# Retention, soft mixture of experts and a gated MLP in one kernel: the weights' place among the loads, and the keys' transposes

## The chip, the cores and the metric

The kernel runs on one core of a Trainium2 chip. The metric is the time of one execution on the device in microseconds (us), the median of three runs. The engines are called PE (TensorE, matrix products and transposes), DVE (VectorE), ACT (ScalarE), POOL (GpSimd) and SP (SyncE, which here issues most DMA loads).

## The reference

Three stages, one feeding the next. A linear attention with decay (4 batches, 8 heads, 768 tokens, 64 columns a head) gives 3072 tokens of 512 columns. A soft mixture of 8 experts with 4 slots each mixes all tokens into 32 slots, runs the experts and mixes back. An MLP of width 2048 follows.

```python
for t in range(S):
    state = gamma * state + einsum('bhd,bhe->bhde', k[:, :, t], v[:, :, t])
    y[:, :, t] = scale * einsum('bhd,bhde->bhe', q[:, :, t], state)
logits = x @ phi
d = softmax(logits, axis=0); slot_input = d.T @ x
slot_out[e] = maximum(slot_input[e] @ w1[e], 0) @ w2[e]
x = softmax(logits, axis=1) @ slot_out
h = x @ w_in
out = (h * sigmoid(1.702 * h)) @ w_out
```

## The kernel before

The order of all work is written out by hand: each engine runs its instructions in the order of the program, and waits only for what it reads or overwrites. Memory comes from pools of tiles; an instruction that takes a tile over waits until its last users are done.

**Chunks.** The tokens are worked in 24 chunks of 128 (6 to a batch). Chunk i has a load of 768 KB (`load_a`: keys, queries and values, tensor kqv) that SP issues in `loads(i - 4)`, four chunks ahead, into one of five rotating buffers; so it also waits until chunk i - 5 has released its buffer (its last product with the queries, L266). The steps of a chunk are `stage_a` (scores, L206), `stage_p` (mask, on DVE), `stage_v` (two products on POOL, vt and tb), and `stage_b`: the output y on PE (L266 and L270), the state (L278, copied by ACT to s_sb), and the product of y and tb on DVE, xT (L282). All chunks share one y tile of two PSUM banks; `stage_b` uses the first 256 columns of each bank. Chunks come in pairs; after `stage_b(i - 1)` of an odd i comes `group(i)`, which holds transposes of earlier chunks (`stage_c`, L291), and in turn logits, softmax statistics and slot sums of four chunks at a time.

**Keys.** For the state the keys are needed the other way round. For most chunks ACT's queue loads them a second time (tensor kt, 256 KB each, `load_b`); for chunks 4, 9, 14 and 19 (`KTP`) PE transposes them in `keys` (called in the groups of i = 3, 9, 13 and 19), into columns 256 to 511 of the y tile's two banks (`keys_tok`, L227), and ACT copies them out (L232). The next `stage_b` writes y anew and so waits for that copy.

**Weights.** The experts' weights are 32 pieces of 1 MB, loaded in the order of their use, some in halves. Among the chunks `loads(i)` asks for as many halves as a quota says, `(i - 1) * 2 * (NW + NQ) // (NI - 1)` with NW = 14, NQ = 3, NI = 24, ahead of the chunk load of the same call; what is left of the 17 pieces is asked for after the last chunk. Six more pieces follow into memory that the chunks release, and nine into buffers that the first expert products release. All are issued by SP in the order of the program. Two loads of the last stage are put among the last pieces (`early_loads`, keyed by the number of pieces left, `WL`): half of the first w_in tile when three are left, and half of the first w_out pair when two are left. Behind the last piece come the second w_in half, the second w_out half, and the next w_in tile.

**Experts and the start of the last stage.** `exp_w1`, `exp_t1`, `exp_w2`, `exp_t2`, `exp_sum` work one pair of experts: two products on PE (L512, L543) with a transpose between, ACT's copy of the result (os, L546), its transposes (tq, L552), ACT's th (L558) and two sums on DVE (A, L561). A feeds `make_gd` (L569), the first product with w_in, and by it all of the last stage. The last stage wants weights in another form: `narrow` makes three DVE operations (L157, L159, L161) of each part that lands, and for w_out `wout_ops` adds a rounding on ACT (L614) and a difference on POOL (L617). `f0_ops` and `f1_ops` are these five for the first two blocks of w_out, `w1_ops` the three for the second half of the first w_in tile; they stand between the expert steps at the places seen in the code.

**phi** (64 KB, for the logits) is loaded from POOL's queue at the start.

Of the kernel before, what the change touches and what calls it, by code (L numbers as in the profile page):

```python
# [24 lines left out]
NI = B * NC  # L25
# [6 lines left out]
CB = {"end": 160}  # L32
NB = NT // 512
NW = 14
NQ = 3
# [11 lines left out]
PAD = 128  # L47
BUD = 2.0
E0 = (1.2, 1.7, 1.7, 1.7, 2.2)
WL = (3, 2)  # L50


@with_exitstack
def retention_soft_moe_mlp(
# [12 lines left out]
    nc = tc.nc  # L67
# [42 lines left out]
    phi = at.tile([P, KDM, NS], F32, name="phi")  # L110
# [12 lines left out]
    def load_half(pool):  # L123
        if half:
            t, src = half.pop()
            nc.sync.dma_start(out=t[:, 2:4], in_=src[:, 2:4])
            return
        kind, e, k = pieces.pop()
        t = pool.tile([P, 4, 512], F32, tag="w", name=f"{kind}_{e}_{k}")
        src = (w1 if kind == "w1" else w2)[e, k, :, 0:2048].rearrange("p (j f) -> p j f", j=4)  # L130
        nc.sync.dma_start(out=t[:, 0:2], in_=src[:, 0:2])
        W[kind, e, k] = t
        half.append((t, src))

    def load_piece(pool, tag="w"):
        kind, e, k = pieces.pop()
        t = pool.tile([P, 4, 512], F32, tag=tag, name=f"{kind}_{e}_{k}")
        src = (w1 if kind == "w1" else w2)[e, k, :, 0:2048].rearrange("p (j f) -> p j f", j=4)
        nc.sync.dma_start(out=t, in_=src)
        W[kind, e, k] = t  # L140

    def load_wout(r, a0=0, a1=2):
        if a0 == 0:
            wo_t[r] = wq.tile([P, 2, DM], U64, tag="w", name=f"wo{r}")
        src = w_out[r].rearrange("p (a d) -> p a d", a=2)
        nc.sync.dma_start(out=wo_t[r][:, a0:a1], in_=src[:, a0:a1])

    def load_win2(j, z, f0=0, f1=256):
        if f0 == 0:
            raw_t[j, z] = wq.tile([P, KDM, 256], U64, tag="w", name=f"wi{j}_{z}")  # L150
        src = w_in[j, :, 1024 * z:1024 * z + 1024].rearrange("p (k f) -> p k f", k=KDM)
        nc.sync.dma_start(out=raw_t[j, z][:, :, f0:f1], in_=src[:, :, f0:f1])
# [135 lines left out]
    def stage_c(i):  # L288
        xp = mt([P, DM], f"xp{i}")
        for a in range(NP):  # L290
            nc.tensor.transpose(xp[:, a * P:(a + 1) * P], xT_t[i][:, a, :], ident)  # L291
        x_t[i] = xp
        if i < NI - 2:
            stage_c2(i)
# [15 lines left out]
    def logits(g):  # L310
        lp = mt([P, P], f"lp{g}")
        js = [range(4)] if g < NG - 1 else [range(3), range(3, 4)]
        for k, j in [(k, j) for js_ in js for k in range(KDM) for j in js_]:
            mm(lp[32 * j:32 * j + 32, :], lhsT=phi[:, k, :], rhs=xT_t[4 * g + j][:, k, :],  # L314
               start=(k == 0), stop=(k == KDM - 1))
        return lp
# [17 lines left out]
    def softmax_stats(g, lp):  # L334
        m, nm = softmax_max(g, lp)
        eT, es = softmax_exp(lp, nm, g)
        al = softmax_scale(g, nm)
        if g < NG - 1:
            keep_logits(g, lp)
        run["m"] = m  # L340
        g_t[g] = (eT, es, al)
# [22 lines left out]
    def stage_g2(g):  # L364
        eT, es, al = g_t[g]
        er = mt([P, 2, P], f"er{g}")
        if g < NG - 2:
            nc.tensor.transpose(er[:, 1], lT_t.pop(g), ident)
        e = exp_tr(g, eT, er[:, 0])
        run_z(es, al, g)  # L370
        g_t[g] = (e, al)
        return er[:, 1]
# [7 lines left out]
    def stage_g3(g):  # L380
        add_op(g, *slot_product(g))
# [28 lines left out]
    def row_softmax(g, rl):  # L410
        lp = rl.rearrange("p (j s) -> p j s", j=4)
        rx = sm.tile([P, 4], F32, tag="rx", name=f"rx{g}")
        nc.vector.reduce_max(out=rx, in_=lp, axis=AX.X)
        ce = sm.tile([P, 4, NS], F32, tag="eT", name=f"ce{g}")
        nc.vector.tensor_tensor(out=ce, in0=lp, in1=rx[:, :, None].to_broadcast([P, 4, NS]), op=ALU.subtract)
        ex = sm.tile([P, 4, NS], F32, tag="ex", name=f"ex{g}", bufs=1)
        nc.scalar.activation(out=ex, in_=ce, func=AF.Exp)
        return ex
# [434 lines left out]
    with tc.manual_schedule():  # L853
# [5 lines left out]
        nc.scalar.dma_start(out=ca_t[:, 0:CA["tab"]], in_=ca[:, 0:CA["tab"]])  # L859
        nc.scalar.dma_start(out=cb_t, in_=cb[:, 0:CB["end"]])  # L860
        nc.scalar.dma_start(out=ca_t[:, CA["tab"]:CA["end"]], in_=ca[:, CA["tab"]:CA["end"]])
        nc.gpsimd.dma_start(out=phi.rearrange("p k s -> p (k s)"), in_=cb[:, CB["end"]:CB["end"] + 128])
        wz = xx.tile([P, NP * P], F32, tag="xT", name="wz", bufs=5)
        nc.vector.memset(wz, 0.0)
        wu = ps.tile([P, NP * P], F32, tag="m", name="wu")
# [6 lines left out]
        ex_t, count = {}, [0]  # L872

        def group(i):
            spare["n"] = 0
            g = (i - 5) // 4
            if i % 4 == 1:
                if g > 0:
                    stage_g3(g - 1)
                lp = logits(g)  # L880
                keys(i)
                softmax_stats(g, lp)
                stage_c(i - 3)
            else:
                if i > 3:
                    spare["n"] = 1
                    rl = stage_g2(g)
                stage_c(i - 3)
                keys(i)
                if 3 < i < NI - 1:  # L890
                    ex_t[g] = row_softmax(g, rl)
            stage_c(i - 2)

        def keys(i):
            for x in (i, i + 1):
                if x in KTP:
                    keys_tok(x, y_p[0])

        def loads(i):
            if i >= NI:  # L900
                return
            while count[0] < (i - 1) * 2 * (NW + NQ) // (NI - 1):
                if i < 6 or half:
                    load_half(wp if count[0] < 2 * NW else wq)
                    count[0] += 1
                else:
                    load_piece(wp if count[0] < 2 * NW else wq)
                    count[0] += 2
            load_b(i + 1)
            for x in range(2 if i == 0 else i + 4, i + 5):  # L910
                load_a(x)

        for i in range(3):
            stage_a(i)
            stage_p(i)
            stage_v(i)
            loads(i)
            if i != 1:
                stage_b(max(i - 1, 0))
        for i in range(3, NI, 2):  # L920
            stage_a(i)
# [52 lines left out]
        xk, xk_e = pool(right, "xk", 2)  # L974
        slotT = xk.tile([P, KDM, NS], F32, name="slotT", bufs=1)
        slot_inputs(sb)
        early_loads = {WL[0]: lambda: load_win2(0, 0, 0, 128), WL[1]: lambda: load_wout(0, 0, 1)}
        while len(pieces) > 1:
            early_loads.get(len(pieces), lambda: None)()
            load_piece(wp)  # L980
        early_loads.get(1, lambda: None)()
        load_half(wp)
        load_half(wp)
        load_win2(0, 0, 128, 256)
        load_wout(0, 1, 2)
        load_win2(0, 1)
# [50 lines left out]
                )  # L1037
        exp_w2(2)
        f0_ops, f1_ops = wout_ops(0), wout_ops(1)
        for fn in f0_ops[0:3]:  # L1040
            fn()
        exp_w2(3, 0, 1)
        exp_sum(2, exp_t2(2))
        for fn in f0_ops[3:5]:
            fn()
        exp_w2(3, 1, 3)
        exp_w2(3, 3, 4)
# [304 lines left out]
```

## Time and profile before

| | us |
|---|---|
| median of three runs | 442.68 |
| the three runs | 442.94, 442.44, 442.68 |
| the profiled execution | 443.33 |
| its span, first to last instruction | 441.6 |
| PE busy | 429.5 |
| DVE busy | 329.5 |
| ACT busy | 213.8 |
| POOL busy | 72.4 |

The profile is of one execution. Busy times are sums over the span; they say how full an engine is, not what ends last at a given point. The chunks take the first 106 us, the experts run to 149 us, and the rest is the last stage. The granted clock of TensorE is full throughout.

### The profile page before, as it was taken

The numbers are of one execution on the slowest core, as the hardware profiler recorded it, in microseconds if no ns is written. First come the engines' busy times: TensorE is split into PE (matmuls) and PEld (weight loads), VectorE is DVE, ScalarE is ACT, GpSimd is POOL, SyncE is SP. The second block draws the span as 40 slices with busy tenths as digits, with TensorE's granted clock in tenths as the row PEclk, the third lists the DMA queues.
The fourth block names the chain that finished last, engine by engine and source line by source line (L and its number), as shares of the span: only waits on it lengthen the run. The fifth ranks groups of instructions, "written<-read, shape, count | busy, mean of one in ns | idle before, by whom it ended". The sixth has DMA issues, their size and how long they took to land.

```text
span 441.6 us, 10084 instructions
## 1 busy us (share of the span) xinstructions
PE 429.5 (97%) x4145; PEld 363.2 (82%) x4145; DVE 329.5 (75%) x627; ACT 213.8 (48%) x392; POOL 72.4 (16%) x83
## 2 busy tenths in 40 slices
PE   7999999989999999999999999999999999999995
PEld 5888888867433687888788879999999999999994
DVE  2547578564476689878968768698889999898835
ACT  2322332313121566566556556665666666665630
POOL 3453434432000123120131120000000000000000
PEclk9999999999999999999999999999999999999999
DMA  8999999999999767845683262402333333312102
GB/s 316 414 394 415 410 411 413 409 414 413 401 412 404 280 208 271 282 177 191 200 182 108 84 96 102 138 31 66 96 97 96 95 96 97 96 39 61 49 0 95
DMA packets 26109, 94.48 MB, mean 214 GB/s; under 512 B 2496, under 2 KB 9920, under 8 KB 20816
## 3 DMA queue, kind: packets, MB, share of 16 engines
q1 hardware_dynamic: 20704, 82.45, 50.0%
q0 software_dynamic: 2784, 7.41, 6.6%
q10 hardware_dynamic: 2576, 3.99, 2.5%
q8 instruction: 32, 0.52, 0.5%
q14 instruction: 13, 0.11, 0.1%
HBM read 79.16 MB, written 14.68 MB: 213 GB/s over the span
## 4 chain that ended last, share of the span: by engine, by line
PE 89%; DMA 8%; DVE 1%; issue 0%; ACT 0%; POOL 0%; SPq 0%; DVEq 0%; POOLq 0%
PE pb L814 32%; PE pb L746 25%; DMA kqv<-kqv_dram 7%; PE y L270 4%; PE sc L206 3%; PE hp L512 3%; PE eo L543 3%; PE pb L788 3%; PE pb L697 2%; PE y L266 2%; PE xp L291 2%; PE lp L314 1%; PE st L278 1%; PE op L393 1%; DMA kqv_first<-kqv_dram 1%; PE pb L579 1%
## 5 line engine op out<-in xcount | busy, mean ns | idle before, releaser
L814 PE MATMUL pb<-wb,ghl 128*128 128x256 f32 x672 | 100.9, 283 | 0.0
L814 PEld LDWEIGHTS pb<-wb,ghl 128*128 128x128 f32 x672 | 89.5, 192 | 0.1
L746 PE MATMUL pb<-wo_hl,gh 128*128 128x512 f32 x288 | 89.5, 395 | 0.0
L814 PE MATMUL pb<-wa,ghl 128*128 128x256 f32 x504 | 78.9, 283 | 0.0
L814 PEld LDWEIGHTS pb<-wa,ghl 128*128 128x128 f32 x504 | 68.7, 192 | 0.0
L746 PEld LDWEIGHTS pb<-wo_hl,gh 128*128 128x128 f32 x288 | 53.8, 188 | 11.8 <-ACT gh L706 0.2
L803 DVE TENSOR_TENSOR ghl<-F,ghl 128x896 fp32r<-128x896 f32 x56 | 60.7, 1084 | 0.0
L791 ACT ACTIVATE F<-pb 128x512 f32<-128x512 f32 x56 | 33.5, 599 | 52.3 <-PE pb L788 52.3
L746 PE MATMUL pb<-wo_hl,gl 128*128 128x512 f32 x144 | 55.9, 395 | 0.3 <-DVE gl L712 0.3
L799 ACT CAST ghl<-F 128x896 fp32r<-128x896 f32 x56 | 52.3, 934 | 0.9 <-DVE F L795 0.8
L712 DVE TENSOR_TENSOR gl<-gg,gh 128x512 fp32r<-128x512 f32 x36 | 24.7, 687 | 14.3 <-ACT gg L707 14.2
L706 ACT ACTIVATE gh<-pb 128x512 fp32r<-128x512 f32 x36 | 21.7, 604 | 26.9 <-PE pb L697 26.4
L793 DVE TENSOR_TENSOR F<-F 128x256 f32<-128x256 f32 x56 | 23.5, 420 | 14.0 <-ACT F L791 13.8
L282 DVE TENSOR_TENSOR xT<-y,tb 128x512 f32<-128x512 f32 x19 | 13.1, 691 | 27.0 <-PE y L270 27.0
L746 PEld LDWEIGHTS pb<-wo_hl,gl 128*128 128x128 f32 x144 | 27.0, 188 | 6.9 <-DVE gl L712 0.7
L280 ACT COPY s_sb<-st 128x256 f32<-128x256 f32 x20 | 7.5, 373 | 50.6 <-PE st L278 46.8
L219 DVE TENSOR_TENSOR pt<-sc,ca_t 128x512 f32<-128x512 f32 x44 | 28.2, 681 | 4.9 <-PE sc L206 4.9
L246 POOL TENSOR_TENSOR tb<-ca_t 128x512 f32<-128x512 f32 x19 | 19.9, 1048 | 42.7 <-DVE xT L282 42.7
L270 PE MATMUL y<-pt,vt 128*64 128x128 f32 x352 | 24.1, 279 | 0.0
L788 PE MATMUL pb<-cT,gst 128*128 128x256 f32 x112 | 22.8, 285 | 0.4 <-ACT gst L594 0.4
L206 PE MATMUL sc<-kqv 64*128 64x128 f32 x288 | 19.6, 281 | 3.0 <-DMA kqv<-kqv_dram 2.7
L270 PEld LDWEIGHTS y<-pt,vt 128*64 128x64 f32 x352 | 18.8, 136 | 3.6 <-issue 2.2
(197 smaller groups left out, 657.6 us busy)
## 6 DMA issues: line engine op xcount, KB each, us to landing
w<-w_dram SPq DMA_DIRECT2D x27, 1024.0 KB, 11.9
kqv<-kqv_dram SPq DMA_DIRECT2D x18, 768.0 KB, 9.9
wi<-w_in_dram SPq DMA_DIRECT2D x7, 1024.0 KB, 5.1
wo<-w_out_dram SPq DMA_DIRECT2D x7, 1024.0 KB, 5.0
scr<-sg POOLq DMA_DIRECT2D x28, 256.0 KB, 4.6
pr<-scr SPq DMA_DIRECT2D x12, 512.0 KB, 4.9
w<-w_dram SPq DMA_DIRECT2D x10, 512.0 KB, 12.5
out_dram<-X SPq DMA_DIRECT2D x10, 512.0 KB, 3.9
```

The lines of the kernel that those rows point to most:

```text
L206: mm(sc[hh][:, a, :], lhsT=kT[hh * D:(hh + 1) * D, a, :], rhs=q_[hh * D:(hh + 1) * D, a, :], start=True, stop=True)
L219: nc.vector.tensor_tensor(out=pt[hh], in0=sc[hh], in1=mask[:, None, :].to_broadcast([P, NP, P]), op=ALU.mult)
L270: mm(out_(a, hh ^ (a & 1)), lhsT=vt[:, 2 * a + (hh ^ (a & 1)), :], rhs=pt[hh ^ (a & 1)][:, a, :], start=(c == 0 and a < 2), stop=True, ski ...
L706: nc.scalar.activation(out=gh, in_=hp, func=AF.Gelu_apprx_sigmoid)
L712: nc.vector.tensor_tensor(out=gl, in0=gg, in1=gh.bitcast(F32), op=ALU.subtract)
L746: mm(acc[t], lhsT=g[:, t * P:(t + 1) * P], rhs=w, start=first and n == 0, stop=n == 2 and (last or final or (u == NSEQ - 2 and t == 3)))
L788: mm(hp[:, 256 * z:256 * z + 256], lhsT=gst[:, (f + z) * P:(f + z + 1) * P], rhs=cT[:, 256 * blocks[e]:256 * blocks[e] + 256], start=z == ...
L791: nc.scalar.activation(out=F[:, 0:4].rearrange("p q t -> p (q t)"), in_=hp, func=AF.Gelu_apprx_sigmoid)
L793: tt(out=F[:, 4:6], in0=F[:, 0, None].to_broadcast([P, 2, P]), in1=F[:, 1:3], op=ALU.subtract)
L799: nc.scalar.copy(out=GHL[k][:, 0], in_=F_[k][:, 1:8])
L803: nc.vector.tensor_tensor(out=GHL[k][:, 1], in0=F_[k][:, 1:8], in1=GHL[k][:, 0].bitcast(F32), op=ALU.subtract)
L814: mm(pv[:, p], lhsT=ghl[:, n // 2, g], rhs=wf[:, n % 2], start=j == j0[e] and n == 0 and i in (4, 0), stop=j == NSP - 1 and n == 2, skip_g ...
```

## The change

Five edits. The quota for weights among the chunks is taken from 15 pieces in place of 17; the pieces left over are asked for after the last chunk, so that their order is the same. phi's load moves from the start to behind the POOL work of chunk 1. In `group`, `keys` is the first step in place of standing after the logits, or after `stage_g2` and the first `stage_c`. The load of the first half of the first w_out pair moves from ahead of the last two expert pieces to behind them. The three DVE operations on it move from ahead of the first part of the last expert product to behind the sum of expert pair 2, where the rounding on ACT and the difference on POOL already stood.

```diff
-WL = (3, 2)
+WL = 3
...
-        nc.gpsimd.dma_start(out=phi.rearrange("p k s -> p (k s)"), in_=cb[:, CB["end"]:CB["end"] + 128])
...
             g = (i - 5) // 4
+            keys(i)
             if i % 4 == 1:
                 if g > 0:
                     stage_g3(g - 1)
                 lp = logits(g)
-                keys(i)
                 softmax_stats(g, lp)
                 stage_c(i - 3)
             else:
...
                 stage_c(i - 3)
-                keys(i)
                 if 3 < i < NI - 1:
...
-            while count[0] < (i - 1) * 2 * (NW + NQ) // (NI - 1):
+            while count[0] < (i - 1) * 2 * (NW + NQ - 2) // (NI - 1):
...
             loads(i)
-            if i != 1:
+            if i == 1:
+                nc.gpsimd.dma_start(out=phi.rearrange("p k s -> p (k s)"), in_=cb[:, CB["end"]:CB["end"] + 128])
+            else:
                 stage_b(max(i - 1, 0))
...
-        early_loads = {WL[0]: lambda: load_win2(0, 0, 0, 128), WL[1]: lambda: load_wout(0, 0, 1)}
+        early_loads = {WL: lambda: load_win2(0, 0, 0, 128)}
         while len(pieces) > 1:
             early_loads.get(len(pieces), lambda: None)()
             load_piece(wp)
-        early_loads.get(1, lambda: None)()
         load_half(wp)
         load_half(wp)
+        load_wout(0, 0, 1)
         load_win2(0, 0, 128, 256)
...
         f0_ops, f1_ops = wout_ops(0), wout_ops(1)
-        for fn in f0_ops[0:3]:
-            fn()
         exp_w2(3, 0, 1)
         exp_sum(2, exp_t2(2))
-        for fn in f0_ops[3:5]:
+        for fn in f0_ops[0:5]:
             fn()
         exp_w2(3, 1, 3)
```

## Rows read from the trace of the kernel before

**Rows 1.** The page, part 1: busy us (share of the span) x instructions.
```profile
PE 429.5 (97%) x4145; PEld 363.2 (82%) x4145; DVE 329.5 (75%) x627; ACT 213.8 (48%) x392; POOL 72.4 (16%) x83
```

**Rows 2.** The waits of PE: who waited for whom, us, times, longest.
```profile
PE sc L206 <- DMA kqv<-kqv_dram: 2.7, 3, 2.2
...
PE y L266 <- ACT kt L232: 0.6, 2, 0.3
```

**Rows 3.** Timeline of PE: start us, us, instruction, idle before and its releaser.
```profile
86.49 0.67 PE L266 MATMUL y<-kqv,s_sb 64*64 64x128 f32 x16 [0.32 <-ACT kt L232]
...
91.90 1.16 PE L206 MATMUL sc<-kqv 64*128 64x128 f32 x16 [2.16 <-DMA kqv<-kqv_dram]
```

**Rows 4.** Windows: busy us by engine; then granted clock, DMA share, GB/s.
```profile
56.00:106.00 50.00, 47.33 (x868) 39.95 (x864) 32.50 (x65) 14.46 (x42) 21.04 (x21) 1.00 1.02 412
104.00:148.00 44.00, 43.61 (x447) 19.19 (x445) 23.92 (x78) 9.86 (x24) 3.31 (x4) 1.00 1.00 403
```

**Rows 5.** Timeline of PE, the instructions at the head of the groups.
```profile
20.20 0.63 PE L227 MATMUL y<-cb_t,kqv_first 128*128 128x128 f32 x4
...
42.90 1.06 PE L393 MATMUL op<-x,e 128*32 128x512 f32 x8
...
59.08 1.06 PE L393 MATMUL op<-x,e 128*32 128x512 f32 x8
...
84.43 0.33 PE L368 MATMUL er<-cb_t,lT 128*128 128x128 f32 x1
```

**Rows 6.** Timeline of DVE, its reads of y before those groups.
```profile
19.43 0.69 DVE L282 TENSOR_TENSOR xT<-y,tb 128x512 f32<-128x512 f32 x1 [2.10 <-PE y L270]
...
42.62 0.69 DVE L282 TENSOR_TENSOR xT<-y,tb 128x512 f32<-128x512 f32 x1 [0.52 <-PE y L270]
...
58.78 0.67 DVE L282 TENSOR_TENSOR xT<-y,ca_t 128x512 f32<-128x512 f32 x1
...
84.08 0.69 DVE L282 TENSOR_TENSOR xT<-y,ca_t 128x512 f32<-128x512 f32 x1 [0.65 <-PE y L270]
```

**Rows 7.** Line 232, 42.9 to 44 us: ACT's wait, ns min/median/max, first and last start.
```profile
L232 ACTq EVENT_SEMAPHORE  x1: 256/256/256, 43.1 to 43.1; - x1
```

**Rows 8.** DMA issues at 63.2, 131.4, 131.9 and 150.1: KB each, us to landing.
```profile
kqv<-kqv_dram SPq DMA_DIRECT2D x1, 768.0 KB, 10.0
...
w<-w_dram SPq DMA_DIRECT2D x1, 512.0 KB, 13.6
...
wi<-w_in_dram SPq DMA_DIRECT2D x1, 512.0 KB, 14.3
...
wo<-w_out_dram SPq DMA_DIRECT2D x1, 1024.0 KB, 4.8
```

**Rows 9.** Timeline of SP, the issues of the first three.
```profile
63.17 0.33 SPq L178 DMA_DIRECT2D kqv<-kqv_dram  x1
...
131.12 0.43 SPq L126 DMA_DIRECT2D w<-w_dram  x1
131.92 0.38 SPq L152 DMA_DIRECT2D wi<-w_in_dram  x1
```

**Rows 10.** Timeline of DVE at the end of the experts.
```profile
142.27 0.42 DVE L157 TENSOR_SCALAR fr<-wo 128x512 uint32<-128x512 uint32 x1
...
143.45 0.69 DVE L161 SCALAR_TENSOR_TENSOR fr<-wo,fr 128x512 uint32<-128x512 uint32 x1
...
146.25 0.55 DVE L157 TENSOR_SCALAR win<-wi 128x512 uint32<-128x512 uint32 x1 [1.23 <-DMA wi<-w_in_dram]
148.43 0.36 DVE L561 TENSOR_TENSOR A<-tq,th 128x64 f32<-128x64 f32 x2 [1.63 <-ACT th L558]
```

**Rows 11.** Timeline of ACT in the same stretch.
```profile
144.54 0.62 ACT L614 CAST wo_hl<-fr 128x512 fp32r<-128x512 f32 x1
146.81 0.85 ACT L546 ACTIVATE os<-eo,zr 128x256 f32<-128x256 f32 x2 [1.66 <-PE eo L543]
```

**Rows 12.** Timeline of PE in the same stretch: the last expert product.
```profile
144.32 2.80 PE L543 MATMUL eo<-w,hT 128*32 128x256 f32 x48
```

## The prediction

> **What bounds the kernel now.** I read the page's first part, then the waits of TensorE (PE), then the windows, then the DMA loads one by one. The page gives PE 429.5 us of a 441.6 us span [rows 1], so a gain has to come out of the 12.1 us in which PE is idle, or out of PE work removed. The change removes none: it reorders. Of the idle time the waits name two kinds that the change touches: 2.7 us in three waits for the chunks' input (kqv), and 0.6 us in two waits for ScalarE's copy of transposed keys [rows 2]. The longest of the first, 2.16 us, stands at 91.9 us, and one of the second, 0.32 us, at 86.5 [rows 3].
>
> The windows show the second limit: the DMA engines are full (share 1.00 to 1.02, 403 to 412 GB/s) from the chunks to 148 us, when the experts end [rows 4]. So up to there bytes land on a timetable that no reordering of the asking speeds up; a transfer can only change places with another. At 412 GB/s a 1 MB piece takes 2.5 us, a half 1.27, a chunk's 768 KB 1.9.
>
> **1. Fewer weights among the chunks' loads.** The quota falls from 34 halves spread over the chunks to 30; by the two formulas chunk 18 is asked for behind 16 halves, not 20, and chunk 22 behind 22, not 26: 2 MB, 5.0 us earlier each. Before, chunk 18 was asked for at 63.17 and landed 10.0 us later [rows 8, 9]. All three kqv waits are shorter than one piece (2.5 us), which is the least that the chunks waited for move up, so all go: **-2.7 us** at PE. Bounds: 0 to -2.7.
>
> What is late next is the queue itself: it may run dry. Chunk 18 is asked for when a buffer comes free, paced by PE. Alone in the queue a 1 MB load took 4.8 us [rows 8], that is 2.3 us of head and 2.5 of transfer; so before, chunk 18 stood behind 10.0 - 2.3 - 1.9 = 5.8 us of transfers once its head was over. With 5.0 us of weights gone and PE some 0.6 us later there (part 2), 0.2 us is left. It may dry up there for 0 to 1.0 us (the upper end: kt loads counted out of the backlog, and chunk 22, just as short of weights); each such us lands everything later by as much. I take **+0.2**, nearer the row's own remainder.
>
> **2. Transposes of keys first.** Keys go into the other half of the y tile that VectorE (DVE) is then reading (L282). In the chunk-9 group ScalarE, which wants that same half, sat 0.256 us on a semaphore from 43.1 [rows 7], until DVE's read of the first half ended at 42.62 + 0.69 = 43.31 [rows 6]; and at 20.20 the transposes started 0.08 us after the read that ended at 20.12 [rows 5, 6]. So the halves aren't free of each other, and keys can't start before that read ends, plus 0.08. Moved to the front, PE would reach them at 42.90, 59.08 and 84.43 [rows 5], and must wait till 43.39, 59.53 and 84.85: +0.49, +0.45, and +0.42 less the 0.32 wait that goes [rows 3] = +0.10. In the first group (20.20) the transposes already sat at the end of the read; nothing changes. Sum **+1.04 us**. If the halves were independent, it would be -0.6 (the two waits of rows 2); I take the first end, since rows 7 shows the wait.
> The Trainium skill (PSUM — Partial Sum Buffer, "PSUM bank collisions raise a hardware error") speaks against this edit: two engines on one bank and quadrant collide even at disjoint columns, so the access has to be guarded by bank. By it the edit costs 1.04 us, without it it gives 0.6; the trace agrees with the rule.
>
> **3. phi asked for after chunk 1.** GpSimd's issue moves behind its vt and tb of chunk 1, 64 KB: 0.16 us of transfer either way, which may put the first chunk's input forward by as much (-0.16) or delay GpSimd's next product, which PE wants microseconds later (0). 0.
>
> So PE comes to the last expert -2.7 + 1.04 = **1.7 us earlier**.
>
> **4. The first output weights behind the last expert weights.** Now each landing counts. Before, the last weight half was asked for at 131.12 and landed 13.6 us later, 144.7; the next load (second w_in part) 131.92 + 14.3 = 146.2 [rows 8, 9]. The edit moves one w_out half behind 2 MB that stood after it. The bytes up to there are the same, so the last weights land at 144.7 - 1.27 = 143.45, and w_out **lands at 144.7** in their old place; w_in stays at 146.2.
> PE wants the last weights for the last third of the 48 matmuls from 144.32 [rows 12], at about 146.1, now 144.4: in time by 1.0 us. That half of the edit is worth nothing but cover.
> The other half is on the path. DVE's three operations on w_out (142.27 to 143.45 + 0.69 = 144.14: 1.87 us, with no wait ahead [rows 10]) can't start before 144.75, and end at 146.62. ScalarE's rounding of the result (L614, 0.62 us [rows 11]) follows to about 147.2. It is now queued on ScalarE **ahead of the copy of the last expert's output** (os, L546), which ran at 146.81, when PE's product came [rows 11]. Behind os queue PE's transposes, th, DVE's sum A at 148.43 [rows 10], the first product with w_in, and the whole last stage. os starts at 147.2: **+0.4 us**, however early PE is. The 1.7 us become PE idle before its transposes of os.
> The move of the three DVE operations behind the sum of expert 2 costs nothing: they fill 144.75 to 146.62, where DVE sat idle 1.23 us for w_in [rows 10], and end 0.4 us after its landing; the first operation on the second w_in part then runs to 147.1, and A comes at 148.8.
>
> **Sum.** +0.4 (part 4) + 0.2 (a dry queue) = +0.6 us; parts 1 and 2 cancel out against the new wait. Behind 149 us the same instructions run in the same order; the next loads there had microseconds to spare. The profiled execution took 443.33 us, 441.6 of it the span, so 443.9 for its like; it lies 0.65 above the median of the three runs (442.68). For the median: 442.68 + 0.6 = **443.3**.
>
> **Rivals.**
> A, **the gain arrives** (faster). If w_out lands 2 us or more before 144.7, ScalarE is free when PE's product comes, and PE's 1.7 us go through. DVE still does the first operation on the second w_in part (0.55 us, at 146.25 when that lands [rows 10]) ahead of A, so A can't start before 146.8 against 148.43: -1.6, 441.1 us. For it: the queue's rate is a mean over 140 us, and 1% of it is 1.4 us. Against: share 1.00 in all windows, and 13.6 us from asking to landing. 0.13.
> The Trainium skill (DMA: Bandwidth & Descriptors, "Latency and other measured facts") has 0.6 us to the first byte for a load that SP issues; by that alone the half would be there by an estimated 133.5 us and A would hold. The 13.6 us of rows 8 are the queue ahead, and decide against it.
> B, **the queue runs dry** (slower). Place: chunk 18 to 22, where 0.2 us of backlog is left. Price: 1 us for each us, for nothing makes the bytes up. From 0.5 us dry on, +0.4 + 0.5 = 0.9 is slower by over 0.2%; at 1.0 to 1.5 us it gives 444.1 to 444.6. For it: buffers are paced by a later PE. Against: kt loads in the same queues fill some. 0.24.
> C, **the stalls stay** (the edit doesn't do what it says): SP asks no sooner because buffers, not weights, hold it. Then PE is 1.04 late from part 2 and nothing hides it: 443.7. Against: chunk 18's 10.0 us are mostly queue. 0.06.
>
> **How the numbers follow.** Forecast 0.57, 442.8 to 443.5. About 0.2% (0.89 us) is what a measurement of this kernel can tell from no change, so the forecast counts as the same: faster 0.13 (A), same 0.57, slower 0.30 (B and C). The range leaves out A's full gain and a long dry spell, and keeps a small gain and most of B: 442.3 to 444.6.
>
> **What would show it.** After: no kqv waits of PE in the chunks (part 1); PE waits of 0.4 to 0.5 us for DVE's xT ahead of L227 at chunks 9, 13, 19 (part 2); DVE's wait for a w_out landing near 144.7, ScalarE's wait for DVE ahead of L614, and a PE idle of 1.5 to 2 us released by os (part 4). DMA share under 1 near 63 us shows B. It would be wrong if w_out lands by 143, or if L614 doesn't hold os.

## The result, and the profile after

The change makes the kernel **slower: 447.18 us** (median of six runs, 446.6 to 449.66) against 442.76 (six runs, 442.36 to 444.87). The ratio is 1.0105, with a 95% interval of 1.0086 to 1.0124. The forecast was 443.3 and its range ended at 444.6, so the time lies 2.6 us outside. The profiled execution is the slowest of the six, 449.66 us with a span of 447.9, 6.3 above that of before; the other five are 1.3 to 3.1 us shorter. What differs among them comes below.

The waits of PE in the changed kernel (who waited for whom: us in all, times, longest us), which answer [rows 2]:

```profile
PE tq L552 <- ACT os L546: 2.7, 1, 2.7
PE y L227 <- DVE xT L282: 1.5, 4, 0.4
...
PE eo L543 <- DMA w<-w_dram: 1.0, 2, 0.6
```

Both waits that the change aimed at are gone, kqv's 2.7 us and the keys' copy's 0.6. Three others stand in their place, 5.2 us together. The first is one wait, at the end of the experts. The timelines there, first PE, then DVE, then ACT (start us, us, instruction, idle before and its releaser), which answer [rows 10 to 12]:

```profile
145.72 1.06 PE L543 MATMUL eo<-w,hT 128*32 128x256 f32 x12 [0.65 <-DMA w<-w_dram]
146.71 0.53 PE L448 MATMUL cp<-csb,cs 128*128 128x128 f32 x4
149.95 1.12 PE L552 MATMUL tq<-cb_t,os 128*128 128x128 f32 x4 [2.71 <-ACT os L546]
...
151.84 2.04 PE L569 MATMUL gd<-win,A 128*128 128x128 f32 x8
```

```profile
146.99 0.43 DVE L157 TENSOR_SCALAR fr<-wo 128x512 uint32<-128x512 uint32 x1 [4.11 <-DMA wo<-w_out_dram]
...
148.18 0.69 DVE L161 SCALAR_TENSOR_TENSOR fr<-wo,fr 128x512 uint32<-128x512 uint32 x1
148.79 0.42 DVE L157 TENSOR_SCALAR win<-wi 128x512 uint32<-128x512 uint32 x1
151.35 0.36 DVE L561 TENSOR_TENSOR A<-tq,th 128x64 f32<-128x64 f32 x2 [2.14 <-ACT th L558]
```

```profile
148.90 0.62 ACT L614 CAST wo_hl<-fr 128x512 fp32r<-128x512 f32 x1 [6.41 <-DVE fr L161]
149.43 0.83 ACT L546 ACTIVATE os<-eo,zr 128x256 f32<-128x256 f32 x2
```

Read from the bottom: ACT's copy os, which PE wants, starts when the rounding L614 is done; L614 waited 6.41 us for DVE; DVE waited 4.11 us for the half of w_out to land, at 147.0. That is the chain which the prediction described, 2.3 us later than it said (144.7). The first product with w_in (gd) starts at 151.84; in the kernel before it started at 148.84, 0.41 behind A [rows 10]. So 3.0 us are lost by then.

The windows show where most of the 2.3 us come from, and a second loss behind 149 us. The columns are those of [rows 4]; the last three are granted clock, DMA share and GB/s. First before, then after:

```profile
20.00:28.00 8.00, 7.75 (x152) 6.85 (x154) 3.89 (x7) 2.33 (x6) 4.10 (x4) 1.00 1.02 400
64.00:76.00 12.00, 11.80 (x226) 10.48 (x224) 9.33 (x16) 2.59 (x7) 6.15 (x6) 1.00 1.02 412
...
104.00:140.00 36.00, 35.62 (x346) 15.31 (x347) 19.02 (x66) 7.60 (x19) 2.03 (x3) 1.00 1.01 408
...
152.00:156.00 4.00, 4.00 (x23) 3.08 (x22) 3.49 (x6) 3.22 (x7) 1.62 (x1) 1.00 0.98 391
```

```profile
20.00:28.00 8.00, 7.79 (x148) 7.03 (x152) 3.78 (x7) 2.22 (x6) 4.10 (x4) 1.00 0.91 343
64.00:76.00 12.00, 12.00 (x232) 10.87 (x230) 8.83 (x16) 3.36 (x9) 6.15 (x6) 1.00 0.98 367
...
104.00:140.00 36.00, 35.62 (x329) 14.32 (x327) 20.73 (x68) 6.52 (x17) 1.24 (x2) 1.00 1.02 415
...
148.00:152.00 4.00, 2.05 (x13) 1.98 (x14) 1.82 (x6) 2.26 (x6) 1.27 (x1) 0.66 0.54 219
152.00:156.00 4.00, 3.27 (x16) 2.88 (x16) 2.64 (x6) 1.66 (x5) 0.00 (x0) 0.50 0.44 139
156.00:160.00 4.00, 4.00 (x15) 3.45 (x15) 2.48 (x4) 2.06 (x5) 1.49 (x1) 0.56 0.90 315
```

From 20 to 28 us 57 GB/s are missing, 456 KB or 1.1 us at the full rate of about 410; from 64 to 76 us 45 GB/s, 540 KB or 1.3 us. Together that is 2.4 us. From 104 to 140 us it moves more than before, 415 against 408 GB/s, which gives 252 KB or 0.6 us back. So the bytes account for 1.8 of the 2.3 us by which w_out is late; where the rest comes from is not shown. The queue ran dry in part, at two places. And from 149 to 160 us the granted clock is at half, the lower of its two levels (1.2 of 2.4 GHz); gd's eight products take 2.04 us where they took 1.16 in the profile before. PE before, and then after:

```profile
148.84 1.16 PE L569 MATMUL gd<-win,A 128*128 128x128 f32 x8
...
154.69 0.46 PE L448 MATMUL pb<-csb 128*128 128x128 f32 x4
```

```profile
160.49 0.46 PE L448 MATMUL pb<-csb 128*128 128x128 f32 x4
```

That product of the next stage (pb) is 5.8 us late, and to the last product (442.08 against 436.26) it stays 5.8. The loss is thus 3.0 us up to gd and 2.8 behind it; the missing 0.5 of the span lies behind the last product.

The issues of chunk 18's input and of the last loads (KB each, us to landing) answer [rows 8]:

```profile
kqv<-kqv_dram SPq DMA_DIRECT2D x1, 768.0 KB, 4.7
...
wo<-w_out_dram SPq DMA_DIRECT2D x1, 512.0 KB, 14.9
wi<-w_in_dram SPq DMA_DIRECT2D x1, 512.0 KB, 14.3
```

Chunk 18's 4.7 us, where it was 10.0, are near what a load takes that is alone in the queue: 4.8 for 1 MB [rows 8], and 2.3 + 1.9 = 4.2 for its 768 KB by the prediction's own working. So some 0.5 us of transfers was left ahead of it. Two stretches of 1 us behind its request (63.89), from the same trace, show how far the rate fell all the same:

```profile
65.00:66.00 1.00, 1.00 (x24) 0.93 (x22) 0.63 (x1) 0.37 (x1) 0.29 (x1) 1.00 0.82 254
...
71.00:72.00 1.00, 1.00 (x24) 0.88 (x18) 1.00 (x2) 0.00 (x0) 0.83 (x1) 1.00 0.84 268
```

### The profile page after: what moved, and what is told of

Read it like the earlier page. It is cut to its first block, busy times and chain, and to the rows that moved or that the text cites. A ratio compares the mean times of both kernels' runs of the same rounds, so it can differ in the third digit from the quotient of the medians.

```text
span 447.9 us, 10092 instructions
## 1 busy us (share of the span) xinstructions
PE 433.8 (97%) x4145; PEld 366.7 (82%) x4145; DVE 329.9 (74%) x627; ACT 214.1 (48%) x392; POOL 72.1 (16%) x83
## 4 chain that ended last, share of the span: by engine, by line
PE 90%; DVE 5%; DMA 3%; issue 1%; ACT 0%; DVEq 0%; ACTq 0%
PE pb L814 32%; PE pb L746 24%; PE y L270 5%; PE sc L206 5%; DMA wo<-w_out_dram 3%; PE pb L788 3%; PE hp L512 2%; PE y L266 2%; PE xp L291 2%; PE pb L697 2%; PE eo L543 2%; PE st L278 1%; PE lp L314 1%; PE op L393 1%; DVE xT L282 1%; PE pb L579 1%
## 5 line engine op out<-in xcount | busy, mean ns | idle before, releaser
L707 ACT ACTIVATE gg<-pb 128x512 f32<-128x512 f32 x36 | 21.6, 601 | 0.1
```

## The experiments

Each is compared with the kernel before on the same chip; experiments 1, 2, 4 and the first of 3 ran on one chip, 5 to 7 and the second of 3 on another, 8 to 11 on a third. The theory after the result: the smaller quota empties the queue, w_out comes 2.3 us later, and the clock falls behind PE's wait for os. Rivals: the rounding's place alone is the fault; the keys' waits are; phi is; the fall has another cause.

**1. a1_rounding_behind_os.** The changed kernel, with rounding and difference of w_out behind the copy os, so that nothing on ACT holds it.

```diff
-        for fn in f0_ops[0:5]:
+        for fn in f0_ops[0:3]:
             fn()
         exp_w2(3, 1, 3)
         exp_w2(3, 3, 4)
+        for fn in f0_ops[3:5]:
+            fn()
```

> The changed kernel, with one thing moved: ACT's rounding of the first w_out block (L614) and POOL's difference stand behind the copy of the last expert's output (os, L546), not ahead of it. Theory (os is held by the rounding, which waits for a w_out half that landed at 147.0): os returns to about 146.8, PE's wait of 2.7 us for os goes, and the next thing late is DVE's sum A, which stands behind three operations on w_out and one on w_in that can't end before 149.2. A at about 149.3 against 151.35, so 1 to 2 us are won even where the clock still falls, and 3 to 3.5 us (443.5 to 444) where it stays full. Rival (the time is lost in the chunks, or to the clock for another reason): no change, 447.

449.09 us (447.15 to 449.78), ratio 1.0132 (1.0106 to 1.0159): no gain at all, where 1 to 2 us were expected. DVE and then PE in its trace:

```profile
149.79 1.33 DVE L157 TENSOR_SCALAR win<-wi 128x512 uint32<-128x512 uint32 x1 [0.95 <-DMA wi<-w_in_dram]
151.05 0.34 DVE L561 TENSOR_TENSOR A<-tq,th 128x64 f32<-128x64 f32 x2
```

```profile
147.05 0.71 PE L552 MATMUL tq<-cb_t,os 128*128 128x128 f32 x4
...
151.44 2.07 PE L569 MATMUL gd<-win,A 128*128 128x128 f32 x8 [3.04 <-DVE A L561]
```

PE's transposes come 2.9 us earlier, at 147.05, but A stands on DVE behind an operation on w_in, which landed late too. Much the same idle time, 3.04 us, now stands ahead of gd and is put down to DVE, and the clock fell here too (gd's products 2.07 us). The prediction's rival A had named that next limit, w_in on DVE ahead of A. The rounding is a carrier of the delay, not its source. How much its place is worth by itself this run can't tell: w_in was there at 149.8, in the changed kernel by 148.8, and the operation on it took 1.33 us in place of 0.42. The rounding also still stood on ACT ahead of th, which started at 149.41.

**2. a2_quota_back.** The changed kernel with the old quota.

```diff
-            while count[0] < (i - 1) * 2 * (NW + NQ - 2) // (NI - 1):
+            while count[0] < (i - 1) * 2 * (NW + NQ) // (NI - 1):
```

> The changed kernel with the old quota of weights among the chunks (17 pieces); phi, keys and the w_out half stay changed. Theory (the queue ran dry at 20 to 28 us and at 64 to 76 us for want of weights, and so w_out landed 2.3 us later than its place in the queue says): DMA share back to 1.00 or more in both stretches, w_out lands at 144.7 to 145.0, PE's waits for kqv return (1.5 to 2.7 us) and take in most of the keys' waits; PE waits for os under 1 us, the clock stays full, 443.1 to 444. Rival (the loads' order at the end is what costs, whatever the quota): w_out still lands near 147 and the time stays at 446 to 447.

444.01 us (443.9 to 445.49), ratio 1.0027 (1.0012 to 1.0042). 64 to 76 us is back at 411 GB/s and 20 to 28 at 379; w_out lands at 145.5, PE waits 1.1 us for os, and the mean clock of every run is 0.997 or more. Its window from 64 to 76 us:

```profile
64.00:76.00 12.00, 12.00 (x236) 10.70 (x232) 8.16 (x15) 4.05 (x13) 6.15 (x6) 1.00 1.02 411
```

Against the kernel before on its own chip 0.9 us are left of the 4.4: this one term brings back 3.5.

**3. a3_pe_kept_busy and a3b_pe_kept_busy_less.** The changed kernel with products of the identity, 20 and then 9 of them, ahead of the transposes of os, so that PE has something to do while it waits. Their results are not used.

```diff
+        wu2 = ps.tile([P, P], F32, tag="st", name="wu2")
+        for _ in range(20):
+            mm(wu2, lhsT=ident, rhs=ident, start=True, stop=True)
         tq = exp_t2(3)
```

> The changed kernel with 20 products of the identity with itself, into a PSUM bank that is free, ahead of the transposes of os: PE works about 2.2 us of the 2.7 us in which it otherwise waits. Nothing else is moved, and os, w_out and all other waits stay where they are. Theory (PE's idle time brings the clock down to half from 149.3 for 5 to 10 us, and that is 1.5 to 3 us of the loss, on top of the 2.6 us by which os is late): granted clock full throughout, 445.3 to 445.8. Rival (the clock falls for another reason, or its fall costs nothing because other engines set the pace there): no change, 446.6 to 447.4.

> The changed kernel with 9 products of the identity with itself ahead of the transposes of os, about 2.1 us by the 0.235 us each that the 20 took; so few that the transposes of os aren't put off. Theory (clock): granted clock full from the start of the experts to the end, and 1.5 to 3 us less than the changed kernel: 444.6 to 445.8. Rival (the clock's fall costs nothing on the path): 446.6 to 447.4.

The first: 448.89 us (448.12 to 450.71), ratio 1.0141 (1.0115 to 1.0167). The products took 4.70 us, longer than the wait, so that they cost 1.3 us themselves: a miss in size. And in the run with the trace w_out came 1.7 us later than in the changed kernel, though the program is the same up to there:

```profile
148.71 0.43 DVE L157 TENSOR_SCALAR fr<-wo 128x512 uint32<-128x512 uint32 x1 [4.03 <-DMA wo<-w_out_dram]
```

There 20 to 28 us moved only 264 GB/s. So how dry the queue runs differs from run to run; the four traces whose programs are alike up to w_out (the changed kernel, experiment 1 and these two) have 264 to 343 GB/s at that place and w_out at 147.0 to 148.7. The mean clock, though, was 0.999 or more in all four runs. The second, with 2.24 us of products: 446.17 us (445.99 to 446.6), ratio 1.008 (1.0067 to 1.0093), clock 0.997 or more in all four. PE in its trace:

```profile
150.23 0.81 PE L552 MATMUL tq<-cb_t,os 128*128 128x128 f32 x4 [0.65 <-ACT os L546]
151.82 1.13 PE L569 MATMUL gd<-win,A 128*128 128x128 f32 x8
...
157.62 0.46 PE L448 MATMUL pb<-csb 128*128 128x128 f32 x4
```

gd starts at 151.82, as in the changed kernel (151.84), and the pace behind it is that of before: the next stage's pb comes 5.8 us behind gd, as in the kernel before, where the changed kernel takes 8.65. With the same 3.0 us lost ahead of gd, the median is 1.0 us below the changed kernel's, and 3.5 below its slowest run. So by this comparison the fall of the clock costs the changed kernel from 0.4 to 3.5 us, in some runs more than in others, and it doesn't come where PE's idle stretch is cut to 0.65 us.

**4. a4_keys_back.** The changed kernel with the transposes of keys in their old places.

```diff
-            keys(i)
             if i % 4 == 1:
...
                 lp = logits(g)
+                keys(i)
...
                 stage_c(i - 3)
+                keys(i)
```

> The changed kernel with the keys' transposes in their old places; quota, phi and the w_out half stay changed. Theory (the four waits for DVE, 1.5 us of PE idle, lie in front of a wait for DMA and are swallowed; PE paced by 1 us less frees the chunks' buffers a little earlier): the waits go, PE's wait for os grows by about as much, w_out lands 0 to 0.7 us earlier, 446.4 to 447.2. Rival (PE's waits in the chunks are on the path to the end): 1.0 to 1.5 us are won, 445.7 to 446.2.

448.0 us (447.28 to 448.44), ratio 1.0118 (1.0101 to 1.0135), clock 0.986 to 0.994. The four waits for xT are gone, the 0.6 us for kt are back, w_out lands at 146.5 and the wait for os is 2.7 us as before. The 1.5 us of waits that part 2 adds are worth nothing in the time. They do matter to the queue:

```profile
64.00:76.00 12.00, 12.00 (x234) 10.69 (x234) 9.77 (x17) 2.68 (x8) 6.16 (x6) 1.00 1.01 407
```

With the keys in their old places the second dry stretch is all but gone, at the same smaller quota; the first stays (20 to 28 us: 330 GB/s). The same shows in experiment 5 (405 and 356), while keys first with the old quota leaves 64 to 76 us full (411 in experiment 2, 412 in 8). Chunk 18 is asked for at 62.94 us here and at 62.30 in experiment 5, against 63.89 in the changed kernel. So the stretch at 64 to 76 us needs both parts, the smaller quota and chunks that are asked for later.

**5. b1_quota_alone.** The kernel before with the smaller quota and nothing else (the line of 2, the other way round).

> The kernel before with the smaller quota and nothing else of the change. Theory (the smaller quota takes PE's waits for kqv away, but leaves the queue too shallow at 20 to 28 us and 64 to 76 us, so all that lands later is 1.3 to 2.3 us late): no kqv waits, GB/s under 380 in those stretches, the last expert weights land at 146 to 147 where PE wants them at 143.4, PE waits for them some 3 us, the second w_in part lands at 147.5 to 148.5 and A comes at 148.1 to 149.1 against 148.43. 442.4 to 443.5 if the clock stays full; 445 to 446 if PE's wait brings it down. Rival (the w_out half's new place is what costs): the time falls by the 2.7 us of kqv waits less what DMA takes back, 441 to 442.

443.39 us (442.97 to 444.1), ratio 1.0019 (1.001 to 1.0028). The waits of PE and two windows in its trace:

```profile
PE eo L543 <- DMA w<-w_dram: 2.4, 2, 1.7
```

```profile
20.00:28.00 8.00, 7.75 (x158) 6.91 (x160) 3.89 (x7) 2.33 (x6) 4.12 (x5) 1.00 0.96 356
64.00:76.00 12.00, 12.00 (x229) 10.27 (x230) 9.77 (x18) 2.75 (x8) 6.56 (x7) 1.00 1.01 405
```

kqv's 2.7 us are gone, and 2.4 us of waits for the experts' weights have come: the chunks' gain turns into a wait for bytes that land on their own timetable. Only the first stretch is short here; the second, expected under 380 GB/s, is nearly full. A came 0.55 us earlier than before in the profiled execution (147.88), and the median shows nothing of it: by the ratio part 1 alone costs 0.8 us (0.4 to 1.2).

**6. b2_wout_alone.** The kernel before with the half of w_out behind the last weights and its three DVE operations behind the sum of expert pair 2 (part 4), nothing else.

```diff
-WL = (3, 2)
+WL = 3
...
-        early_loads.get(1, lambda: None)()
         load_half(wp)
         load_half(wp)
+        load_wout(0, 0, 1)
...
-        for fn in f0_ops[0:3]:
-            fn()
         exp_w2(3, 0, 1)
         exp_sum(2, exp_t2(2))
-        for fn in f0_ops[3:5]:
+        for fn in f0_ops[0:5]:
```

> The kernel before with the w_out half and its three DVE operations moved as in the change, and quota, phi and keys as before. Theory (the rounding on ACT holds os; with a full queue w_out lands at 144.7): w_out at 144.7 to 145.0, os at 147.2, PE waits 0.4 to 0.7 us for it, clock full, +0.4 to +0.7, 443.1 to 443.5. Rival (this edit is what costs the 4.4 us): 446 to 447.

446.17 us (444.27 to 446.95), ratio 1.0072 (1.0052 to 1.0092). DVE and then ACT in its trace, of the run that took 444.27:

```profile
144.84 0.43 DVE L157 TENSOR_SCALAR fr<-wo 128x512 uint32<-128x512 uint32 x1 [0.62 <-DMA wo<-w_out_dram]
```

```profile
146.76 0.62 ACT L614 CAST wo_hl<-fr 128x512 fp32r<-128x512 f32 x1 [2.93 <-DVE fr L161]
147.29 0.83 ACT L546 ACTIVATE os<-eo,zr 128x256 f32<-128x256 f32 x2
```

w_out landed at 144.8 and os started at 147.29, where the prediction had 144.7 and 147.2; gd came at 149.30, 0.46 later than before. So the sum for part 4, +0.4, holds to 0.1 us. But that run has a mean clock of 0.998; the others, at 0.996, 0.990 and 0.991, took 445.51, 446.82 and 446.95. So the landing and os came as the theory had them, and the time came out as the rival had it: this part alone costs 3.5 us in the median. PE waited 1.03 us for os in the run with the trace, and the clock stayed. The other three have no trace; that the clock fell at the same place, and behind a wait of the same length, is likely but not shown.

**7. c2_late_cut_alone.** The kernel before with the quota cut by one piece, and from chunk 17 on only.

```diff
-            while count[0] < (i - 1) * 2 * (NW + NQ) // (NI - 1):
+            while count[0] < (i - 1) * 2 * (NW + NQ) // (NI - 1) - (2 if i > 16 else 0):
```

> The kernel before with the quota cut by one piece only from chunk step 17 on, where the one long kqv wait (2.16 us) comes from, and untouched where the queue ran shallow; nothing else of the change. Theory (what spoils the smaller quota is the queue running shallow, not the cut itself): DMA full at 20 to 28 and 64 to 76 us, the 2.16 us wait gone, PE 2.16 us earlier at the experts, a wait of 0.5 to 1 us for the last weights (144.7), then A held by the second w_in part on DVE till 146.8: 1.3 to 1.7 us won, 441.0 to 441.6, clock full. Rival (weights asked for later land later, whatever the queue's depth, and PE only waits in another place): 442.5 to 443.2.

**442.12 us** (441.49 to 443.48, 12 runs), ratio 0.9984 (0.9973 to 0.9996): a small gain, the only one here, and the best of all kernels run. It lies between the theory's times and the rival's.

```profile
20.00:28.00 8.00, 7.74 (x164) 6.91 (x166) 3.89 (x7) 2.25 (x5) 4.12 (x5) 1.00 1.02 407
64.00:76.00 12.00, 11.64 (x222) 10.32 (x220) 9.23 (x17) 2.58 (x7) 6.15 (x6) 1.00 1.02 412
```

The queue stays full at both places, kqv's waits fall from 2.7 to 0.6 us, and A comes at 146.96, 1.47 us before that of before [rows 10]. In the median less than half of that is left: by the ratio 0.7 us (0.2 to 1.2).

**8. b3_keys_alone.** The kernel before with part 2 alone.

> The kernel before with part 2 alone: the transposes of keys first in their group, quota and output weights as before. Theory (a PE delay among the chunks is swallowed, since the bytes land on a timetable of their own): PE's two kt waits (0.6 us) go, three or four waits for DVE's xT of 0.3 to 0.5 us come, the kqv waits shrink from 2.7 to about 1.7 to 2.2 us, the last expert's sum A comes within 0.4 us of before; 442.4 to 443.2 us, ratio within 0.2% of 1. Rival (each us of PE counts, as the prediction's +1.04 was first reckoned): kqv waits stay 2.7 and A comes 1 us later, 443.6 to 443.9.

442.7 us (442.37 to 443.85, 10 runs), ratio 0.9998 (0.9984 to 1.0012). Its waits of PE:

```profile
PE y L227 <- DVE xT L282: 1.5, 4, 0.4
...
PE sc L206 <- DMA kqv<-kqv_dram: 0.3, 1, 0.3
```

PE loses 1.5 us to DVE and has 0.3 us at kqv in place of 2.7: it comes later to chunks that land when they did, and A is 0.1 us later than before (148.52). Not all of the 2.4 us need be the keys' doing: two more traces whose chunks are those of the kernel before have 1.6 us (experiment 6) and 1.4 (experiment 9) at kqv. Experiments 5 and 8 are two sides of one thing: up to the experts' end the bytes set the time, and PE's gains and losses are slack.

**9. e1_os_copied_again.** The kernel before, with the second half of os written seven times in place of once, so that PE has to wait for it as long as in the changed kernel, while all DMA stays as it was.

```diff
-                nc.scalar.activation(out=os_[:, n * z:n * z + n], in_=op, func=AF.Copy, scale=zr)
+                for _ in range(7 if ep == 3 and z == 1 else 1):
+                    nc.scalar.activation(out=os_[:, n * z:n * z + n], in_=op, func=AF.Copy, scale=zr)
```

> The kernel before with one thing added: ScalarE writes the second half of the last expert's output (os) seven times over instead of once, the same values each time, six copies of 0.41 us = 2.46 us. PE's transposes of os then wait some 2.4 us, about as long as in the changed kernel (2.71), while the quota, the keys, the output weights and the DMA timetable stay those of before. Theory (the wait itself makes the granted clock fall, and the fall costs 1 to 3 us more): PE waits 2 to 2.5 us for os near 149.5, the granted clock of the windows behind it goes to 0.5 to 0.7 for some us in the profiled run, mean clock .985 to .995; 446 to 448 us. Rival (the fall has another cause, such as the DMA timetable or the late w_in, and the wait costs its own length): clock full, 445.0 to 445.4 us. Second rival (the wait is hidden, A being held by w_in or by DVE anyway): under 444 us.

448.61 us (446.5 to 450.26), ratio 1.0121 (1.008 to 1.0162). The eight writes of os take 3.89 us where the two took 0.85 [rows 11], so the added copies are 3.04 us, not the 2.46 expected. PE came to the end of the experts 0.8 us earlier in this run, and A came 2.47 us later than before (150.90); but the time grew by 5.8. ACT and PE, then two windows behind them:

```profile
145.99 3.89 ACT L547 ACTIVATE os<-eo,zr 128x256 f32<-128x256 f32 x8 [1.66 <-PE eo L543]
```

```profile
149.93 0.69 PE L553 MATMUL tq<-cb_t,os 128*128 128x128 f32 x2 [2.93 <-ACT os L547]
```

```profile
148.00:152.00 4.00, 2.07 (x13) 2.08 (x14) 1.07 (x4) 3.12 (x8) 0.00 (x0) 0.73 0.16 61
152.00:156.00 4.00, 3.27 (x21) 2.80 (x21) 2.68 (x5) 1.91 (x5) 0.00 (x0) 0.85 0.56 188
```

The clock falls here too, and the run-to-run order follows it: 446.5 at a mean clock of 0.995, 448.32 at 0.990, 448.89 at 0.988, 450.26 at 0.984. With experiment 3 this shows the cause: a wait of PE of nearly 3 us at this place brings the clock down, with DMA and loads as they were before, and it stays up when PE is kept busy in the wait.

**10. a5_phi_back.** The changed kernel with phi's load at the start again.

> The changed kernel with part 3 undone: phi asked for at the start again. Theory (phi's place is worth nothing): the stretch 20 to 28 us moves 330 to 360 GB/s as in the changed kernel, the wait for os stays 2.7 us, 446.5 to 448 us, within 0.2% of the changed kernel. Rival (phi behind chunk 1 is what leaves the queue dry at 20 to 28 us or makes PE's start late): 20 to 28 us back at 400 GB/s and the last loads 1 us earlier, 444.5 to 446.

448.35 us (447.92 to 448.77), ratio 1.0118 (1.0091 to 1.0144). The two stretches move 368 and 382 GB/s, still short, and the wait for os is 2.7 us. Its mean clock, 0.986 to 0.994, lies where that of the changed kernel lies (0.987 to 0.994). phi is no cause; whether its move gives a few tenths can't be told from this.

**11. a6_late_cut.** The changed kernel with the quota of c2_late_cut_alone.

> The changed kernel with another cut of the quota: that of before, less one piece from chunk 17 on alone, so that chunks 8 to 16 are asked for behind as many weights as before. Theory (the dry stretches are what makes w_out late, one near 22 us and one near 68): 20 to 28 us back at 390 GB/s or more, 64 to 76 at 405 or more, no kqv wait over 0.7 us; w_out's half lands at 144.8 to 145.6, PE waits 1 to 1.8 us for os; 443.3 to 443.9 where the clock stays, 444.5 to 446 where it falls behind that wait. Rival (the moved w_out half is late by its place alone, the dry stretches matter little): w_out at 146.5 or later, 446.5 to 448.

446.1 us (442.96 to 447.3, 10 runs), ratio 1.0056 (1.0031 to 1.0081). The profiled run's windows and ACT:

```profile
20.00:28.00 8.00, 8.00 (x164) 7.23 (x166) 3.78 (x7) 2.31 (x5) 4.02 (x5) 1.00 1.02 406
64.00:76.00 12.00, 11.63 (x222) 10.39 (x218) 8.58 (x15) 3.61 (x10) 6.15 (x6) 1.00 1.02 412
```

```profile
147.03 0.83 ACT L546 ACTIVATE os<-eo,zr 128x256 f32<-128x256 f32 x2
```

With the queue full w_out lands at 144.6, and os starts 2.4 us earlier than in the changed kernel. The ten runs fall apart: three of a mean clock of 1.0 took 442.96 to 443.42, one of 0.998 took 444.49, and six of 0.990 to 0.995 took 446.08 to 447.3. So one and the same program takes either the time of the kernel before or some 3 us more. Only a run of the first kind has a trace (443.32 us; PE waits 1.2 us for os, and the clock stays). How long PE waited in the other runs is not on record, and the landing of w_out does vary from run to run (experiment 3). The Trainium skill (TensorE: Matmul & The Clock Gate, the table "Terms") puts the penalty at the throttled time times the share of clock that is missing. By that rule an estimate for a run of 444.5 us span at a mean of 0.991 is 4.0 us; the runs show about 3. Why they show less is not shown.

## Why the prediction was wrong

Two terms of the sum failed: the dry queue, which had +0.2 us and measured some 2.2, and the clock, which had no term. Either by itself leaves the range: with the dry queue and the clock kept up the median is 446.17 (experiment 3, second), with a full queue and a low mean clock in six of ten runs 446.1 (experiment 11).

**Part 1, the stalls: right.** All kqv waits are gone, and the first expert product starts at 111.52 in place of 113.67: 2.15 us earlier, where -2.7 + 1.04 = -1.7 was forecast. The 2.7 were one execution's, though: 1.6 and 1.4 in two more (experiments 6 and 9). Experiment 5 shows that this gain was slack, as the sum had it: it cancels against a later wait.

**Part 1, the queue: a step that failed.** It had 0.2 us, with 1.0 as the upper end, for one place, chunks 18 to 22. The mechanism is the prediction's rival B and its place was half right; the size was off tenfold: w_out came 2.15 us later than with a full queue (146.99 against 144.84 in experiment 6). At chunk 18 the remainder came out near what was worked out, some 0.5 us. What didn't follow is that a remainder of that size keeps the queue full: 64 to 76 us is 1.3 us of bytes short, by the smaller quota and the later PE together (experiment 4). The other 1.1 us are missing at 20 to 28 us, a place the prediction has no term for: the quota is a straight line through all chunks and takes weights out early too. The windows read for it began at 56 us [rows 4]. The remainder of 0.2 us was a difference of three numbers of 2 to 6 us each, and the range gave it far too little; how dry the queue runs also differs by more than that from run to run (experiment 3). A dry queue was priced at 1 us for each us, and that nearly holds: 1.8 us of bytes short by 140 us, w_out 2.2 us late. What it then does to PE is more, which the point on the clock has.

**Part 2, keys first: right in mechanism, and nearly in size.** The waits for xT came, 0.33 to 0.40 us in each of four groups, where 0.42 to 0.49 in three was forecast and none in the first. Alone they leave the time as it was (ratio 0.9998, experiment 8); with the smaller quota they help to dry the queue at 64 to 76 us (experiment 4).

**Part 3, phi: nothing**, as far as experiment 10 can tell.

**Part 4: right to 0.1 us by itself** in the landing, the rounding and os (experiment 6), but not in the time, which grew by 3.5 us in the median. The last weights, forecast in time by 1.0 us, came late with the dry queue (1.0 us of waits of PE), which the wait for os hides. In the changed kernel the rounding is what the late landing works through, but it is not the only way: with the rounding behind os, w_in holds A to nearly the same time (experiment 1).

**The clock: the other step that failed, a term that was missing.** "Behind 149 us the same instructions run in the same order" was true, and they ran at half the clock for up to 10 us. The prediction itself forecast 1.7 us of PE idle at that place, and gave it no price beyond its length; the profile before showed a full clock throughout, behind a wait of 2.16 us too [rows 3]. So even with a full queue its 443.3 holds only in the runs in which the clock stays: 442.96 to 443.42 in three of ten runs of experiment 11. The median there is 446.1, outside the range as well.

The sum as the runs give it, for the profiled execution of the changed kernel against that of before (+6.3 us): part 4 alone +0.46 (gd, experiment 6); w_out later still, 146.99 against 144.84, +2.15; slower transposes of os at the lower clock and what follows up to gd +0.4; half clock behind gd +2.8; end of the program +0.5. For the median (+4.4) the rest is likely to be less: four of the six runs have a mean clock of 0.993 or 0.994, against 0.987 in the profiled one. How late w_out was in them is not on record.

What stays open is when the clock falls. In the traces it fell in or behind every wait of 2.7 to 3.0 us at this place (the changed kernel, experiments 1, 4, 9 and 10) and behind none of 1.03 to 1.23 (experiments 6, 2 and 11), nor behind one of 2.16 us among the chunks of the kernel before. But three of the four runs of experiment 6 and six of the ten of experiment 11 are long at a low mean clock and have no trace, and the seven of experiment 2 all kept it; these ran on three chips, so that the chip may have a part. A few runs of the kernel before show a mean clock of 0.994 to 0.996 too (443.4 to 444.9 us), also without a trace.

## What to carry to other kernels

Before loads are taken out of a queue that sets the timetable, look at its backlog at every place where the cut bites, the early ones too, and cut only where there is a load's latency to spare: one piece from chunk 17 on gave 0.7 us, two pieces over all chunks cost 0.8 by themselves and 3.5 in the changed kernel. Two parts that look harmless alone, as the quota and the keys did at 64 to 76 us, have to be tried together as well. Idle time that a change collects in one stretch of PE, even where it replaces several shorter waits, can cost several times its length through the clock: allow for that, or put work into it. When a chain of several limits stands close together, moving one of them out of the way (experiment 1) shows the next and no gain.

## What the runs showed of the hardware

- One wait of PE of 2.7 to 3.0 us was followed by half clock (0.50) in all five traces that have one, for up to 10 us. What it costs beside the wait differs from run to run: in experiment 9 from 0.7 to 4.5 us (446.5 to 450.26 against 442.77 + 3.04 of added copies). The runs of such a kernel are spread over 3 to 4 us (446.6 to 449.66 for the changed kernel, 446.5 to 450.26 in experiment 9).
- Products whose result nobody reads kept the clock up in all eight runs of experiment 3 (mean 0.997 or more), and 2.24 us of them were worth 1.0 us in the median.
- A DMA share of 0.98 over 12 us looks full, but it moved 367 GB/s where 1.02 moved 412: of the two columns the GB/s tells of a dry queue.
- A load's landing is not a fixed time: w_out landed at 147.0 to 148.7 us in four traces whose programs are the same up to there, with 264 to 343 GB/s at 20 to 28 us.
